# Other orders for the attention's steps, units and loads, a fourth buffer for k, and six units looked at, in a planned attention-and-MLP kernel

## The chip, the core and the metric

The kernel runs on one core of a Trainium2 chip. The metric is the device time of one execution in microseconds (us). A core has a matrix engine (TensorE, PE in the rows), a vector engine (VectorE, DVE), an activation engine (ScalarE, ACT), a general engine (GpSimd, POOL) and a sequencer that issues the transfers here (SyncE, SP). Each takes its own instructions in a fixed order, and waits on semaphores for the others and for DMAs.

## The reference

A decayed linear attention over 2 batches, 8 heads, 768 tokens of 64 numbers is followed by two MLP layers on 1536 tokens of 512 numbers:

```python
for b in range(nb):                         # blocks of the sequence
    intra = einsum('bhic,bhjc->bhij', qb, kb) * Dmask
    intra = einsum('bhij,bhjd->bhid', intra, vb)
    inter = einsum('bhid,bhde->bhie', qb * lam_pow, kv_state)
    out[:, :, sl] = intra + inter
    kv_state = lam_block * kv_state + einsum('bhsd,bhse->bhde', kb * rev_pow, vb)
x = out, heads side by side                 # 1536 x 512
g = x @ w_gate                              # 512 -> 1536
x = (g * sigmoid(g) * (x @ w_val)) @ w_out  # 1536 -> 512
h = x @ w_in                                # 512 -> 2048
return (h * cos(h)) @ w_out2                # 2048 -> 512
```

The MLP's weights are stored as float64.

## The kernel before

**Attention.** The tokens are taken in 12 chunks of 128 (6 for each batch), all heads at once. For chunk g TensorE runs these steps, built in `att_sub` (L1054): `t` transposes q and k in 64-row halves (L1079, 16 small matmuls); `s` makes the scores (L1097); `d` makes this chunk's share of the state from k and v (L1104); `a` multiplies masked scores with v (L1110); `c` adds the part from the state (L1119). `m` builds the decay mask once. Between them, ScalarE copies the transposes to `qkt` and the results to `xh`, VectorE multiplies the scores with the mask (`at`) and makes `xl`, the rest of x behind the rounding to `xh`, and GpSimd decays k (`kd`), q (`qd`) and the state (`stmp`). Chunks 5 and 11 need no `d`.

**MLP.** Every matmul of it is done as three, on high and low parts (`mm3`, L154 to L156). A `unit` is one of 12 x 512 columns: `gate` or `val`, a block of 512 tokens (0 to 2), and a slice f of the weights (`up_sub`, L1252). For f from 2 on, and for the second layer, blocks are done by a scheme of seven products (`product_sub`, L1281), in the order b, c, a, d, 2, 3, 4 (q and r for four 256x512 quarters of blocks 0 and 1; h and w for block 2, half as wide). Product d goes on in the PSUM bank of product c, after ScalarE has copied c out of it (`copy_job`, L1199). A `down` is a product with the second weight matrix, four pieces of three matmuls each (`down_subs`, L1474). Weights pass from DMA (`raw`) through ScalarE (`ct`) and VectorE (shift L198, join L205) to their parts `wh` (ScalarE) and `wl` (VectorE).

**Orders.** A planner, run when the kernel is built, gives each engine its next instruction by its own estimated times. During the attention TensorE's order is fixed by the string `STEPS` (L53), in which `u` stands for the next unit. After that `next_pe` (L623) takes the first piece of a down, or one of the first `LOOK` pieces of the list of units and products (L629), whichever can start soonest by its estimate. The loads of q, k, v and of the first weight slices (`G` gate, `V` val) are issued by SP in the order of `LOADS` (L58), as far as buffers (`BUFS`, L63) are free. `FETCHES` (L51) and `ATT_NS` (L49) are estimates alone. Where the planner expects TensorE to wait over 1000 ns in the attention, it puts zero matmuls (`zero`, L232; about one for each 115 ns) before the step. The list of units (L298) begins with gate of blocks 0 and 1, then val of both.

Of the kernel before, what the change touches and what calls it, by code (L numbers as in the profile page):

```python
# [26 lines left out]
GBUFS = (5, 0)  # L27
SBUFS, ZBUFS = (6, 1), 2
UNIT_BANKS = 2, 4
LOOK = 4  # L30
ZERO, ZERO_FROM = 115, 1000
COLD, COLD_TO = 215, 7500
KEPT = 4
# [14 lines left out]
EARLY = 4  # L48
LATENCY = 130  # L49
ISSUE = 400  # L50
STALL, FETCHES = 1000, (13000, 20600, 29000, 36500, 45000, 54500, 63500)  # L51
BEHIND = 7000
ATT_NS = {"t": 470, "mask": 700, "s": 892, "st": 464, "av": 875, "qs": 440}  # L53
TILES = {"mask": "32", "t": "64*128", "s": "64*128", "st": "128*64", "av": "128*64", "qs": "64*64"}
STEPS = (
# [3 lines left out]
)  # L59
LOADS = (  # L60
    "q0 k0 k1 q1 q3 k2 q4 q2 k3 q5 v0 k4 k6 k5 v1 v2 q6 k7 v3 v4 G0 v5 k8 q7 v6 q8 "
    "v8 v7 k9 q9 q10 k10 k11 q11 V0 v9 v11 v10 V1 G1"
)  # L63
HELD = 6, 7, 8, 9
BUFS = {"q": 3, "k": 3, "v": 5, "qkt": 2, "qd": 3, "kd": 2, "at": 2, "stmp": 2}
WARM = 4, 5


# [4 lines left out]
def kernel(  # L73
# [222 lines left out]
    ]  # L296
    first2 = len(downs)
    units = [(nm, blk, f) for f in range(GROUP1) for nm in ("gate", "val") for blk in range(NBLK - 1)]  # L298
    units += [(nm, NBLK - 1, f) for f in range(GROUP1) for nm in ("gate", "val")]
    parts = "bcad234"  # L300

# [45 lines left out]
    def matrix(kind, f):  # L347

        if kind in "qh":
            return tuple((nm, f) for nm in ("gate", "val", "sa", "sb"))  # L350
        return ("in2", f), ("in2", f + 1), ("ta", f), ("tb", f)

    def work(op):

        if op[0] in ATT_NS:
            return ATT_NS[op[0]] / 1360
        if op[0] in ("h", "w"):
# [14 lines left out]
    at, todo = 0, list(downs)  # L372
# [40 lines left out]
    for key in list(first_use):  # L413
        if key[0] in ("sa", "sb", "ta", "tb"):
            m = matrix("q" if key[0] in FIRST else "r", key[1])
# [18 lines left out]
    def up_mm(ps, nm, f, x):  # L434
# [15 lines left out]
        "ct": [(0, i) for i in range(CT)], "stage": [(0, i) for i in range(STAGE)], "ring": [(0, i) for i in free if i not in HELD],  # L450
        **{nm: [(0, i) for i in range(n)] for nm, n in BUFS.items()},
    }
# [148 lines left out]
    def turning():  # L601

        return "plain2" in when and ("r", 0, "3") not in when
# [3 lines left out]
    def switch(sub):  # L607

        kind = sub["op"][0]
        if TILES.get(kind) != last_tiles[0]:  # L610
            return SWITCH.get(kind, 145)
        return 60 if last_tiles[1] and kind not in ATT_NS else 0

    def small(sub):

        return sub["op"][0] in ("h", "w")
# [6 lines left out]
    def next_pe():  # L623
# [3 lines left out]
        if pe_att:  # L627
            ahead_ = min(ahead_, key=lambda e: e[1][0]["clock"]),
        for unit, subs in ahead_ if pe_att else ((False, pe_downs[:1]), (True, pe_units[:TURN[1] if turning() else LOOK])):  # L629
            for sub in subs:  # L630
# [12 lines left out]
    def run_pe(sub, end, idle):  # L643

        unit = any(sub is s for s in pe_units)
        last_small[0] = small(sub)
        last_tiles[:] = TILES.get(sub["op"][0]), sub["op"][0] in ATT_NS
        for subs in (pe_att, pe_units, pe_downs):
            subs[:] = [s for s in subs if s is not sub]
        items = []  # L650
        for _ in range(int(sub["bank"])):
# [3 lines left out]
            if unit:  # L655
                unit_banks.add(item[1])
        sub["fn"](*(items or [None]), **({"idle": idle} if idle and sub["op"][0] in ATT_NS and items else {}))
        for key in sub["keys"]:
# [395 lines left out]
    def att_sub(op):  # L1054
# [92 lines left out]

        return dict(ns=ATT_NS[kind], needs=needs, keys=[], bank=n, fn=fn, then=then, clock=seen[op], op=op)

# [513 lines left out]
```

## Time and profile before

| what | us |
|---|---|
| median of 3 runs (lowest, highest) | 591.8 (591.25, 592.13) |
| the profiled execution | 590.59 |
| its span | 588.8 |
| TensorE busy in the span | 578.5 (98%) |
| VectorE busy | 506.0 (86%) |
| ScalarE busy | 362.5 (62%) |
| GpSimd busy | 34.1 (6%) |

Busy time is a sum over the whole span. The attention takes about the first 64 us, and its loads hold the DMA engines busy for most of it; after that TensorE, VectorE and ScalarE work on the MLP alone. Where an engine waits is read from the list of waits and from the timeline, in which an idle time before an instruction stands in brackets with the engine that ended it.

### The profile page before, as it was taken

The page shows a single profiled execution, that of the slowest core. Times are in us where ns is not written, and L with a number is a line of the kernel's source. Part 1 is how long each engine was busy: PE and PEld are TensorE (multiplying, and loading weights), DVE is VectorE, ACT ScalarE, POOL GpSimd, SP SyncE. Part 2 cuts the span into 40 slices and gives each one's busy share as a digit, 9 for nine tenths or more (in the row PEclk, how much of TensorE's full clock was granted, in tenths as well). Part 3 has the DMA queues.
Part 4 walks back from the last instruction along what each step waited for, and adds up shares of the span by engine and source line. Part 5 has one row for each costly group of instructions (what it writes and reads, how often), then busy time and mean ns, then how long its engine had stood idle before and what let it go on. Part 6 is the DMA issues. An engine that isn't in the chain of part 4 may idle for free.

```text
span 588.8 us, 9643 instructions
## 1 busy us (share of the span) xinstructions
PE 578.5 (98%) x3620; PEld 491.8 (84%) x3620; DVE 506.0 (86%) x943; ACT 362.5 (62%) x689; POOL 34.1 (6%) x50
## 2 busy tenths in 40 slices
PE   8999999999999999999999999999999999989997
PEld 5888888888888888888888888888888888868886
DVE  4688899878889889786979999969799999999973
ACT  3554767757567557454453679876568667857641
POOL 5646000000000000000000000000000000000000
PEclk9999999999999999999999999999999999999999
DMA  9999362554585554543441522301212031300013
GB/s 189 211 210 212 113 147 71 162 144 147 175 225 185 156 146 140 170 128 141 129 142 51 180 89 72 107 2 39 70 37 71 1 108 37 108 0 1 1 74 141
DMA packets 72816, 66.68 MB, mean 113 GB/s; under 512 B 40002, under 2 KB 60738, under 8 KB 72770
## 3 DMA queue, kind: packets, MB, share of 16 engines
q1 hardware_dynamic: 72768, 66.07, 40.2%
q8 instruction: 28, 0.46, 0.3%
q14 instruction: 18, 0.15, 0.1%
q10 hardware_dynamic: 2, 0.00, 0.0%
HBM read 54.00 MB, written 12.06 MB: 112 GB/s over the span
## 4 chain that ended last, share of the span: by engine, by line
PE 84%; DVE 11%; ACT 2%; DMA 1%; issue 1%; SPq 0%; ACTq 0%; DVEq 0%
PE bank L154 21%; PE bank L155 21%; PE bank L156 20%; PE bank L1493 5%; PE bank L1494 5%; PE bank L1495 5%; DVE s L529 2%; DVE sum L529 2%; PE bank L1110 2%; PE bank L1097 2%; DVE wl L541 1%; DMA v<-in_v_dram 1%; PE bank L1119 1%; PE bank L1079 1%; PE bank L1104 1%; DVE s L1241 1%
## 5 line engine op out<-in xcount | busy, mean ns | idle before, releaser
L154 PE MATMUL bank<-xl,wh 128*128 128x512 f32 (+1 forms) x336 | 118.4, 352 | 3.0 <-ACT s L536 3.0
L536 ACT ACTIVATE s<-s 128x512 f32<-128x512 f32 (+2 forms) x124 | 73.4, 594 | 75.2 <-DVE s L529 47.5
L155 PE MATMUL bank<-xh,wh 128*128 128x512 f32 (+1 forms) x336 | 117.7, 350 | 0.0
L156 PE MATMUL bank<-xh,wl 128*128 128x512 f32 (+1 forms) x336 | 117.3, 349 | 0.0
L536 ACT ACTIVATE s<-bank 128x512 f32<-128x512 f32 (+2 forms) x126 | 62.5, 500 | 36.4 <-PE bank L156 30.8
L536 ACT ACTIVATE gh<-s 128x512 fp32r<-128x512 f32 x84 | 52.7, 628 | 38.7 <-DVE s L529 35.3
L529 DVE TENSOR_TENSOR s<-bank,s 128x256 f32<-128x256 f32 (+1 forms) x102 | 57.3, 563 | 22.2 <-PE bank L156 21.3
L154 PE MATMUL bank<-wl,gh 128*128 128x512 f32 (+1 forms) x196 | 75.6, 386 | 0.0
L155 PE MATMUL bank<-wh,gh 128*128 128x512 f32 (+1 forms) x196 | 75.6, 386 | 0.0
L156 PE MATMUL bank<-wh,gl 128*128 128x512 f32 (+1 forms) x196 | 75.5, 385 | 0.0
L154 PEld LDWEIGHTS bank<-xl,wh 128*128 128x128 f32 x336 | 63.6, 189 | 12.7 <-ACT s L536 3.7
L156 PEld LDWEIGHTS bank<-xh,wl 128*128 128x128 f32 x336 | 63.6, 189 | 8.4
L155 PEld LDWEIGHTS bank<-xh,wh 128*128 128x128 f32 x336 | 63.7, 190 | 8.1
L529 DVE TENSOR_TENSOR sum<-bank,sum 128x512 f32<-128x512 f32 (+1 forms) x97 | 63.2, 681 | 8.1 <-PE bank L156 5.8
L536 ACT ACTIVATE wh<-ct 128x512 fp32r<-128x512 f32 x91 | 55.5, 627 | 23.8 <-DVE ct L205 20.2
L541 DVE TENSOR_TENSOR wl<-ct,wh 128x512 fp32r<-128x512 f32 x91 | 61.3, 688 | 6.9 <-ACT wh L536 6.2
L529 DVE TENSOR_TENSOR gl<-s,gh 128x512 fp32r<-128x512 f32 x84 | 57.7, 689 | 6.3 <-ACT gh L536 5.9
L1493 PE MATMUL bank<-gh,wl 128*128 128x512 f32 x144 | 56.2, 390 | 0.0
L1494 PE MATMUL bank<-gh,wh 128*128 128x512 f32 x144 | 56.2, 390 | 0.0
L1495 PE MATMUL bank<-gl,wh 128*128 128x512 f32 x144 | 56.1, 389 | 0.0
L193 ACT ACTIVATE ct<-raw 128x512 f32<-128x512 f32 x68 | 44.9, 668 | 7.6 <-DMA raw<-in_moe_w_out_dram 4.4
L205 DVE SCALAR_TENSOR_TENSOR ct<-ct,raw 128x512 int32<-128x512 int32 x68 | 46.4, 689 | 3.1 <-ACT ct L193 1.3
(169 smaller groups left out, 1034.7 us busy)
## 6 DMA issues: line engine op xcount, KB each, us to landing
raw<-in_moe_w_out_dram SPq DMA_DIRECT2D x28, 512.0 KB, 3.6
raw<-in_moe_w_in_dram SPq DMA_DIRECT2D x16, 512.0 KB, 3.8
raw<-in_moe_w_gate_dram SPq DMA_DIRECT2D x24, 256.0 KB, 4.6
raw<-in_moe_w_val_dram SPq DMA_DIRECT2D x24, 256.0 KB, 4.5
draftout<-raw SPq DMA_DIRECT2D x9, 512.0 KB, 2.6
q<-in_q_dram SPq DMA_DIRECT2D x12, 256.0 KB, 5.2
k<-in_k_dram SPq DMA_DIRECT2D x12, 256.0 KB, 5.3
v<-in_v_dram SPq DMA_DIRECT2D x12, 256.0 KB, 5.7
```

Source lines behind the costliest of these rows:

```text
L154: nc.tensor.matmul(ps, wh, xl, start=first, stop=False, **kw)
L155: nc.tensor.matmul(ps, wh, xh, start=False, stop=False, **kw)
L156: nc.tensor.matmul(ps, wl, xh, start=False, stop=last, **kw)
L193: nc.scalar.activation(t, words[:, :, 1].bitcast(F32), AF.Prelu, scale=2.0 ** -112, alpha=2.0 ** 32)
L205: nc.vector.scalar_tensor_tensor(out=w, in0=w, scalar=3, in1=lo, op0=ALU.logical_shift_left, op1=ALU.bitwise_or)
L529: engine, 66 + n * 1.047 if engine == "DVE" else n * 2.45, lambda: unit.tensor_tensor(out=out, in0=in0, in1=in1, op=op),
L536: return go("ACT", (175 if fn == AF.Silu else 40) + n * 0.94, lambda: nc.scalar.activation(out, src, fn, **kw))
L541: return "any", {"DVE": 66 + n * 1.047, "POOL": n * 2.45}, lambda e: (nc.vector if e == "DVE" else nc.gpsimd).tensor_tensor(out=out, in0=i ...
L1097: nc.tensor.matmul(ps[:, p * C:(p + 1) * C], kt[r, p, :], qt[r, p, :], start=True, stop=True)
L1493: nc.tensor.matmul(ps, lo[:, cs], gh, start=first, stop=False)
L1494: nc.tensor.matmul(ps, hi[:, cs], gh, start=False, stop=False)
L1495: nc.tensor.matmul(ps, hi[:, cs], gl, start=False, stop=last)
```

## The change

`BUFS` gives k four buffers; `LOOK` is six; the first four units become gate and val of block 0, then gate and val of block 1, all with f = 0; `STEPS`, `LOADS` and the estimates have other values. No instruction is added or taken away on VectorE, ScalarE or GpSimd; TensorE has 25 zero matmuls in two places of the attention instead of 26 in one, beside 14 at its start in both.

```diff
-LOOK = 4
+LOOK = 6
...
-STALL, FETCHES = 1000, (13000, 20600, 29000, 36500, 45000, 54500, 63500)
+STALL, FETCHES = 1000, (12560, 18624, 25014, 34517, 41507, 53380, 61826, 69630)
...
-ATT_NS = {"t": 470, "mask": 700, "s": 892, "st": 464, "av": 875, "qs": 440}
+ATT_NS = {"t": 490, "mask": 700, "s": 892, "st": 464, "av": 875, "qs": 440}
...
-    "t0 m s0 t1 a0 t2 s1 d0 s2 d1 a1 t3 t4 a2 s3 d2 c2 c1 d3 a3 d4 c3 t5 s4 t6 s5 "
-    "a4 s6 a5 c4 c5 t7 a6 d6 u s7 t8 d7 d8 a7 t9 s8 c7 s9 t10 a8 u c8 t11 s10 a9 d9 "
-    "s11 c9 u d10 a10 a11 c10 c11"
+    "t0 m s0 t1 t2 s1 a0 d0 s2 t3 d1 a1 c1 a2 s3 t4 c2 a3 d2 d3 t5 s4 c3 s5 d4 a4 "
+    "t6 u c4 t7 s6 a5 s7 d6 c5 a6 a7 d7 c7 u u t8 u t9 s8 u t10 s9 d8 a8 t11 s10 "
+    "d9 a9 s11 u c8 c9 a10 d10 a11 c10 c11"
...
-    "q0 k0 k1 q1 q3 k2 q4 q2 k3 q5 v0 k4 k6 k5 v1 v2 q6 k7 v3 v4 G0 v5 k8 q7 v6 q8 "
-    "v8 v7 k9 q9 q10 k10 k11 q11 V0 v9 v11 v10 V1 G1"
+    "q0 k0 k1 q2 q1 v0 k2 q3 k4 k3 v1 v2 q4 v3 k5 q5 G0 v4 q6 k6 v5 k7 q7 V0 v6 v7 "
+    "k9 v9 k8 q8 G1 q10 k10 q9 v8 k11 q11 V1 v11 v10"
...
-BUFS = {"q": 3, "k": 3, "v": 5, "qkt": 2, "qd": 3, "kd": 2, "at": 2, "stmp": 2}
+BUFS = {"q": 3, "k": 4, "v": 5, "qkt": 2, "qd": 3, "kd": 2, "at": 2, "stmp": 2}
...
+    units[:4] = [(nm, blk, 0) for blk in range(2) for nm in ("gate", "val")]
```

The order of SP's first loads before (they are q0, k0 and k1, q1, k2, q2 and q3, v0 and v1, q4, k3 and k4, v2, q5):

```order
L936 DMA q<-in_q_dram 128x8x64
L936 DMA k<-in_k_dram 128x8x64 x2
L936 DMA q<-in_q_dram 128x8x64
L936 DMA k<-in_k_dram 128x8x64
L936 DMA q<-in_q_dram 128x8x64 x2
L936 DMA v<-in_v_dram 128x8x64 x2
L936 DMA q<-in_q_dram 128x8x64
L936 DMA k<-in_k_dram 128x8x64 x2
L936 DMA v<-in_v_dram 128x8x64
L936 DMA q<-in_q_dram 128x8x64
```

And in the change (q0, k0 and k1, q2 and q1, v0, k2, q3, k3, v1, k4, v2, q4):

```order
L937 DMA q<-in_q_dram 128x8x64
L937 DMA k<-in_k_dram 128x8x64 x2
L937 DMA q<-in_q_dram 128x8x64 x2
L937 DMA v<-in_v_dram 128x8x64
L937 DMA k<-in_k_dram 128x8x64
L937 DMA q<-in_q_dram 128x8x64
L937 DMA k<-in_k_dram 128x8x64
L937 DMA v<-in_v_dram 128x8x64
L937 DMA k<-in_k_dram 128x8x64
L937 DMA v<-in_v_dram 128x8x64
L937 DMA q<-in_q_dram 128x8x64
```

v0 moves from the eighth place to the sixth, k2 from the fifth to the seventh and q1 from the fourth to the fifth; further on v3, q5, the two loads of G0 and v4 hold places 14 and 16 to 19, and V0, G1 and V1 stand earlier than before among the rest.

ScalarE late in the second layer, before: `s_5886<-bank5_5827` copies product c of f = 12 (r_c_12 below) out of its bank; the two `gh` rows ahead of it round results that VectorE has multiplied.

```order
L1245 ACTIVATE s_5710<-s_5710,halfpi_86 128x512
L536 ACTIVATE wh_5855<-ct_5825 128x512
L536 ACTIVATE s_5768<-s_5768 128x512
L536 ACTIVATE s_5867<-s_5699 128x512
L1245 ACTIVATE s_5768<-s_5768,halfpi_86 128x512
L536 ACTIVATE gh_5870<-s_5710 128x512
L536 ACTIVATE gh_5887<-s_5768 128x512
L536 ACTIVATE s_5886<-bank5_5827 128x512
```

The same copy in the change is `s_5790<-bank0_5782`:

```order
L193 ACTIVATE ct_5793<-raw_5547 128x512
L537 ACTIVATE s_5778<-s_5405 128x512
L537 ACTIVATE s_5790<-bank0_5782 128x512
L537 ACTIVATE gh_5791<-s_5678 128x512
L537 ACTIVATE s_5694<-s_5694 128x512
```

The copy moves ahead of the next `gh`; on TensorE the products between r_c_12 and r_d_12 change from w_d, w_2, r_a and w_3 to eight pieces of downs and r_a.

## Rows read from the trace of the kernel before

**Rows 1.** Page part 1: busy us (share of span) x instructions.
```profile
PE 578.5 (98%) x3620; PEld 491.8 (84%) x3620; DVE 506.0 (86%) x943; ACT 362.5 (62%) x689; POOL 34.1 (6%) x50
```

**Rows 2.** Waits of TensorE: line, releaser, us in total, times, longest.
```profile
PE bank L154 <- ACT s L536: 3.0, 2, 2.9
PE bank L1110 <- DMA v<-in_v_dram: 1.5, 1, 1.5
PE bank L1097 <- ACT qkt L536: 1.2, 3, 0.6
PE bank L234 <- DVE halfpi L1602: 1.1, 1, 1.1
PE bank L1088 <- DVE skewed L269: 0.2, 1, 0.2
```

**Rows 3.** Timeline of TensorE in the attention: start, us, line, operation, idle before.
```profile
9.16 3.01 PE L234 MATMUL bank<-zeros 128*128 128x256 bf16 x26
13.62 1.09 PE L1110 MATMUL bank<-at,v 128*64 128x128 f32 x16 [1.45 <-DMA v<-in_v_dram]
14.65 0.46 PE L1079 MATMUL bank<-anti,q 64*128 64x64 f32 x8
15.19 1.11 PE L1097 MATMUL bank<-qkt 64*128 64x128 f32 x16
16.24 0.69 PE L1104 MATMUL bank<-v,kd 128*64 128x64 f32 x16
...
28.15 1.11 PE L1097 MATMUL bank<-qkt 64*128 64x128 f32 x16
```

**Rows 4.** Timeline of SP's issues: start, us, what, how many.
```profile
3.81 1.22 SPq L936 DMA_DIRECT2D k<-in_k_dram  x1
5.07 2.20 SPq L936 DMA_DIRECT2D q<-in_q_dram  x2
...
21.99 1.05 SPq L936 DMA_DIRECT2D k<-in_k_dram  x1
```

**Rows 5.** Page part 6: issues, KB each, median us to landing.
```profile
k<-in_k_dram SPq DMA_DIRECT2D x12, 256.0 KB, 5.3
v<-in_v_dram SPq DMA_DIRECT2D x12, 256.0 KB, 5.7
```

**Rows 6.** Timeline of TensorE: a unit alone among steps, and the step after it.
```profile
57.43 0.50 PE L154 MATMUL bank<-xl,wh 128*128 128x512 f32 x1
...
60.38 0.69 PE L1104 MATMUL bank<-v,kd 128*64 128x64 f32 x16
```

**Rows 7.** Timelines of VectorE, ScalarE and TensorE around the longest wait.
```profile
514.37 1.13 DVE L529 TENSOR_TENSOR s<-bank,s 128x512 f32<-128x512 f32 x2
515.42 0.68 DVE L541 TENSOR_TENSOR wl<-ct,wh 128x512 fp32r<-128x512 f32 x1
516.02 0.68 DVE L529 TENSOR_TENSOR s<-s 128x512 f32<-128x512 f32 x1
...
516.74 0.63 ACT L536 ACTIVATE gh<-s 128x512 fp32r<-128x512 f32 x1 [0.81 <-DVE s L529]
517.27 0.58 ACT L536 ACTIVATE s<-bank 128x512 f32<-128x512 f32 x1
...
517.90 0.50 PE L154 MATMUL bank<-xl,wh 128*128 128x512 f32 x1 [2.86 <-ACT s L536]
```

**Rows 8.** Windows: stretch, us; busy (x) of PE, PEld, DVE, ACT, POOL; PEclk, DMA, GB/s.
```profile
66.60:88.40 21.80, 21.80 (x98) 18.04 (x97) 21.59 (x41) 15.45 (x29) 0.00 (x0) 1.00 0.57 144
...
453.60:512.70 59.10, 59.10 (x302) 50.58 (x301) 57.83 (x105) 40.98 (x75) 0.00 (x0) 1.00 0.20 63
...
60.40:101.50 41.10, 41.10 (x251) 34.44 (x251) 40.19 (x76) 29.92 (x55) 0.00 (x0) 1.00 0.43 116
...
500.00:585.00 85.00, 82.14 (x411) 69.90 (x411) 73.40 (x126) 50.48 (x91) 0.00 (x0) 1.00 0.15 53
585.50:588.80 3.30, 0.00 (x0) 0.00 (x0) 0.37 (x1) 0.00 (x0) 0.00 (x0) 0.89 0.18 61
```

## Prediction, made before the change was timed

> **What bounds the kernel now.** I read the page's busy shares first. TensorE is busy for 578.5 of 588.8 us, 98% [rows 1], so the change can win little but TensorE's own waits, and VectorE at 86% is the one other engine close enough to make new ones. Then the list of TensorE's waits [rows 2]: 1.45 us for v0, 1.2 us for ScalarE's copies of the transposes in three places, 3.0 us for a ScalarE copy in two places (2.9 of it in one), and 1.3 us at the start that no edit touches. The timeline of the attention adds what the list can't show [rows 3]: ahead of a0 stand 26 zero matmuls, 3.01 us, that compute nothing, 0.116 us each. Waits and zeros after the first steps together are 3.01 + 1.45 + 1.2 + 3.0 = 8.7 us; that is the most the change could give. Last, the windows [rows 8]: from 60.4 to 101.5 us VectorE is busy for 40.19 of 41.10 us, and before the long wait, 453.6 to 512.7, for 57.83 of 59.10. In these two places VectorE, not TensorE, is what a new order can run into.
>
> **The front: steps and loads.** a0 waited because v0 was the eighth load. In the change it is the sixth, and t2 and s1 come ahead of a0. What counts now is k2, the seventh load. I take the n-th load of the change to be issued when the n-th was before, and to land after the median of its kind. The seventh was issued in the second half of a row from 5.07 that lasts 2.20 us, so at about 6.2 [rows 4], and lands at 6.2 + 5.3 = 11.5 us [rows 5]. On TensorE t1 began before at 9.16 - 0.59 = 8.57 (a t takes 0.54 to 0.59; 14.65 to 15.19 [rows 3]). Now q1 is the fifth load, issued at 3.81, landing at 9.1: t1 starts 0.5 us later. Then 15 zeros (1.74 us) run to 9.1 + 0.59 + 1.74 = 11.4, and t2 starts at 11.5 with 0.1 us of wait.
>
> From there to the next zeros I compare sets of steps. Before, t2 starts at 14.65 and s4 at 28.15: 13.5 us, with 0.6 us of waits in it (1.2 less the longest, 0.6, which comes later). The change's steps from t2 to s5 are the same set plus s4, s5 and a0, less d4: with s 1.05 (15.19 to 16.24), a 1.03 (13.62 to 14.65) and d 0.6 (a bit under its 0.69), 13.5 - 0.6 + 2.1 + 1.0 - 0.6 = 15.4 us. s5 ends at 26.9. There the change has 10 zeros, 1.16 us, ahead of d4, to 28.1; v4 is the nineteenth load (two of G0 stand before it), issued at 21.99, landing at 21.99 + 5.7 = 27.7. The zeros cover it. Each other load of the stretch lands within about half a microsecond of its step by the same count, on either side (v2: issued near 13.2, landing at 18.9; a2 due at 18.4), so I take 0.5 us for small waits, between 0 and 1.6. The waits for `qkt` (1.2 us) go: between each t and its s the new string has at least two other steps, and on ScalarE's queue the copies stand ahead of the copies of x, which were what held them. A fourth k buffer takes away the wait of k3's load for GpSimd's kd0; that is worth nothing by itself while the transfers are what is full.
>
> The units cost something. One alone among small steps takes 60.38 - 57.43 = 2.95 us [rows 6]; in a row, 21.8 / 8 = 2.72 [rows 8]. Before there were three lone ones and the run that ends the attention, now five runs and the last: 2 x 0.23 = 0.46 us. They also move VectorE's work on them forward, into the stretch before 60 us where it is less full; I count that as cover, not as gain.
>
> Sum of the front: gone 3.01 + 1.45 + 1.2 = 5.7; new 0.5 + 1.84 + 1.16 + 0.5 + 0.46 = 4.5. Gain 1.2 us, between -0.3 (all small waits at their upper end, and half of the `qkt` waits kept) and 1.8.
>
> **The long wait: LOOK and the order of products.** The chain of this wait is in three timelines [rows 7]. Product w_3 of f = 12 is done at about 514.8. VectorE then runs the sum of w_3, a `wl` and a multiply (514.37 to 516.70, back to back); ScalarE's `gh` needs the multiply and starts at 516.74; behind it in ScalarE's order stands the copy of r_c_12's bank (517.27), and r_d_12, which goes on in that bank, starts at 517.90 after 2.86 us. The copy itself needed nothing: r_c_12 was long done. It stood behind a `gh`. In the change the copy stands right behind r_c_12's end in ScalarE's order, ahead of the next `gh`, and on TensorE eight pieces of downs and r_a, 8 x 0.68 + 1.36 = 6.8 us, lie between r_c_12 and r_d_12 (0.68 and 1.36 are 3 and 6 matmuls of 2.72 / 12). So this wait goes. What is late next is VectorE: in the order of the change, from the end of down (1, block 2, f = 7) to the multiply that frees the bank for r_a_12, 101 VectorE instructions stand. 81 of them have 512 columns, 0.60 us each (515.42 to 516.02 [rows 7]); 20 are half as wide or shifts, 0.34 by their share of that: 55.4 us. TensorE has 57 us of matmuls in the same stretch. I find no stretch in the second layer with less than 1 us to spare, so I take 0.2 us of wait there, up to 1.5 if VectorE loses what it lost before (59.10 - 57.83 = 1.3). Gain 2.86 - 0.2 = 2.7; the small wait of 0.1 stays.
>
> **The stretch after the attention.** With six looked at, the products h_b, h_c, h_a of f = 2 come before the first downs, so q_2 of f = 2 is due 4.5 us earlier in time (3.4 of it by order, 1.1 by the front). By the order, VectorE has 4.0 us less to do before it (67.9 us in all instead of 71.9). Since VectorE is full there [rows 8], 0.5 us of its spare is used. Before, TensorE never waited for it there [rows 2]; how much was to spare these rows don't tell. I take no cost, and up to 1 us if its first 60 us hold more idle time than before.
>
> **Sum.** 1.2 + 2.7 = 3.9, less 0.1 for that last risk: 3.8 us. The profiled execution took 590.59 us, 1.8 us more than its span, 1.2 us under the median; from 590.59 it gives 586.8, and for the median 591.8 - 3.8 = 588.0.
>
> **Rivals.**
> 1. The front gives nothing: loads land later than my count and the small waits reach their upper end. For it: the loads are paced so that each lands at its step. Against it: with the fourth buffer k3 is issued without waiting. Time 588.0 + 1.5 = 589.5.
> 2. The long wait only moves: VectorE has 55.4 of 57 us to do, and losing 3 us there in place of 1.3 makes r_a_12 wait 1.7 us or more; with a second such place, the whole 2.7 come back. Against it: the copy no longer depends on VectorE. Time 588.0 + 2.7 = 590.7.
> 3. Slower: a load in the middle of the queue waits for its buffer, and SP, which issues in order, holds all behind it. The place is q11 (its buffer is q8's, free after t8), with v11, v10 and the first gate slice of f = 2 behind; and v4. TensorE then waits at d4, t9 or t11. It decides from 3.8 + 1.2 = 5 us of new waits, about four loads' worth (36 loads of the front lie in some 50 us). For it: nothing in the attention covers a wait. Against: t8 is due near 47 and q11's place near 46, so 2 us at most. Time from 593.0 on, 594 taken.
> 4. The clock. Granted clock is 1.00 (2.4 GHz) in the window that holds the wait of 2.86 us, and 0.89 over the 3.3 us after the last matmul, so it falls to the lower level (1.2 GHz) only behind longer idleness [rows 8]. If v4 left TensorE idle beyond 2.86 us, 1.7 us more than planned, the first unit at half the clock would cost 2.95 us more, and little is left of the gain: 588.0 + 1.7 + 2.95 = 592.7. The Trainium skill (TensorE: Matmul & The Clock Gate, Part 1, "What's actually happening") says that the slow clock is the default and only activity lifts it; by that rule fewer zeros speak against this change. The trace agrees that idleness brings the fall, but shows none after 2.86 us.
>
> **Chances.** Forecast 0.62 (586.8 to 589.0); rival 1 0.15; rival 2 0.13; rival 3 0.06; rival 4 0.04. The range has to leave out no more than 2 in 10: from 586.4 (front at its best) to 590.8, which takes in rivals 1 and 2. About 0.2%, 1.2 us, is what a measurement of this kernel can tell from no change: faster is below 590.6, slower above 593.0. Forecast, rival 1 and a third of rival 2 are faster: 0.81; two thirds of rival 2 and half of rival 4 the same: 0.11; the rest slower: 0.08.
>
> **What would show it.** Right: the zeros before t2 end at 11 to 12 us with almost no wait; TensorE's list has no entry over 1 us but the start; the last of the twelve units ends near 87.2 instead of 88.4; r_d_12 without a wait. Wrong: a wait for DMA at d4, a2, t9 or t11 over 1 us (rivals 1 and 3); a wait for VectorE at r_a_12 or in the first 20 us after the units (rival 2); a granted clock under 1.00 before the last matmul (rival 4).

## The result, and the profile after

| | median, us | lowest to highest | runs |
|---|---|---|---|
| before | 591.96 | 591.25 to 592.46 | 4 |
| the change | 586.72 | 586.43 to 587.32 | 4 |

The ratio is 0.9911, with a 95% interval of 0.9895 to 0.9926: 5.2 us less, where 3.8 were predicted. The two profiled executions, 590.59 and 586.67 us, differ by 3.9 us. So the medians moved 1.3 us further than the profiles, and the experiments have to say why.

The page of the change, part 1 (as [rows 1]):

```profile
PE 578.7 (99%) x3619; PEld 491.2 (84%) x3619; DVE 502.9 (86%) x943; ACT 364.3 (62%) x689; POOL 34.5 (6%) x50
```

Its list of TensorE's waits (as [rows 2]):

```profile
PE bank L234 <- DVE halfpi L1603: 1.1, 1, 1.1
PE bank L1080 <- DMA q<-in_q_dram: 0.6, 1, 0.6
PE bank L1111 <- DMA v<-in_v_dram: 0.4, 1, 0.4
PE bank L1089 <- DVE skewed L269: 0.2, 1, 0.2
```

TensorE is busy for as long as before, 578.7 against 578.5 us, in a span that is 4.1 us shorter. The waits of [rows 2] for ScalarE, 3.0 us in the MLP and 1.2 in the attention, are gone; what is left after the start are 1.0 us for two loads. Behind the attention the list has nothing.

TensorE in the attention of the change (start, us, line, operation, idle before), beside [rows 3]; the last row is the first product of f = 2, q_b_2, right behind the twelve units:

```profile
9.69 1.81 PE L234 MATMUL bank<-zeros 128*128 128x256 bf16 x15
11.43 0.46 PE L1080 MATMUL bank<-anti,q 64*128 64x64 f32 x8
...
22.15 1.09 PE L1111 MATMUL bank<-at,v 128*64 128x128 f32 x16 [0.40 <-DMA v<-in_v_dram]
...
24.81 0.53 PE L1080 MATMUL bank<-anti,q 64*128 64x64 f32 x8 [0.63 <-DMA q<-in_q_dram]
...
28.16 1.27 PE L234 MATMUL bank<-zeros 128*128 128x256 bf16 x10
29.35 0.69 PE L1105 MATMUL bank<-v,kd 128*64 128x64 f32 x16
...
34.74 0.67 PE L1120 MATMUL bank<-qd,state 64*64 64x128 f32 x16
...
88.15 0.39 PE L154 MATMUL bank<-xl,wh 128*128 128x512 f32 x1
```

t2 starts at 11.43, s5 ends at 28.16, d4 starts at 29.35, and the units end at 88.15, where they ended at 88.40 before [rows 8]. In this execution the front won 0.2 us.

ScalarE's copy of r_c_12's bank in the change, and r_d_12 on TensorE, which answer to [rows 7]:

```profile
505.02 0.60 ACT L537 ACTIVATE s<-bank 128x512 f32<-128x512 f32 x1
505.51 0.62 ACT L537 ACTIVATE gh<-s 128x512 fp32r<-128x512 f32 x1
...
511.62 0.39 PE L154 MATMUL bank<-xl,wh 128*128 128x512 f32 x1
```

The copy is done 6 us before r_d_12 needs it, and r_d_12 follows its forerunner without a gap.

The last matmul on TensorE, before and in the change:

```profile
585.13 0.28 PE L156 MATMUL bank<-wh,gl 128*128 128x256 f32 x1
...
580.91 0.28 PE L156 MATMUL bank<-wh,gl 128*128 128x256 f32 x1
```

So the profiles' 3.9 us are: 0.2 at the front, 3.0 of waits in the MLP, and 1.0 that nobody had counted: from the start of q_b_2 to the start of the last matmul, less the waits, TensorE takes 493.7 us before (585.13 - 88.40 - 3.0) and 492.8 in the change (580.91 - 88.15). From there to the end, and outside the span, the change takes 0.3 us longer.

### The profile page after: what moved, and what is told of

Read it like the earlier page. It is cut to its first block, busy times and chain, and to the rows that moved or that the text cites. A ratio compares the mean times of both kernels' runs of the same rounds, so it can differ in the third digit from the quotient of the medians.

```text
span 584.7 us, 9694 instructions
## 1 busy us (share of the span) xinstructions
PE 578.7 (99%) x3619; PEld 491.2 (84%) x3619; DVE 502.9 (86%) x943; ACT 364.3 (62%) x689; POOL 34.5 (6%) x50
## 4 chain that ended last, share of the span: by engine, by line
PE 97%; DMA 1%; DVE 1%; POOL 0%; issue 0%; DVEq 0%
PE bank L154 25%; PE bank L156 24%; PE bank L155 24%; PE bank L1495 6%; PE bank L1494 6%; PE bank L1496 6%; PE bank L1098 2%; PE bank L1111 2%; DMA q<-in_q_dram 1%; PE bank L1080 1%; PE bank L1120 1%; PE bank L1105 1%; PE bank L234 1%; POOL powers L266 0%; PE bank L1089 0%
## 5 line engine op out<-in xcount | busy, mean ns | idle before, releaser
L530 DVE TENSOR_TENSOR sum<-bank,sum 128x512 f32<-128x512 f32 (+1 forms) x97 | 62.9, 681 | 11.5 <-PE bank L156 8.9
L530 DVE TENSOR_TENSOR s<-bank,s 128x512 f32<-128x512 f32 (+1 forms) x102 | 57.1, 563 | 16.6 <-PE bank L156 14.7
```

Source lines behind the costliest of these rows:

```text
L530: engine, 66 + n * 1.047 if engine == "DVE" else n * 2.45, lambda: unit.tensor_tensor(out=out, in0=in0, in1=in1, op=op),
```

## Experiments

### Each part alone

The kernel before with `LOOK = 6` alone:

```diff
-LOOK = 4
+LOOK = 6
```

> The kernel before with LOOK = 6 and nothing else changed. Theory (LOOK is what takes the long wait away): ahead of r_d_12 TensorE has w_4 of f = 12 (256 columns) and r_b of f = 14 more than before, 2.1 us of products, so that its wait of 2.86 us falls to about 0.7; the attention keeps its 26 zeros and its waits for v and qkt. 1.5 to 2.1 us faster than before, about 590.2. Rival (the order of units and steps took it away, and LOOK is worth nothing): the wait stands as long as it was or stands elsewhere, 592.0 within 0.6.

Measured: 588.48 us (588.23 to 588.62), before 592.4 when timed beside it, ratio 0.9944 (0.9926 to 0.9963). The place of the long wait on TensorE:

```profile
517.80 0.50 PE L154 MATMUL bank<-xl,wh 128*128 128x512 f32 x1 [0.78 <-ACT s L536]
```

The wait is 0.78 us, as the 2.1 us of products put ahead of r_d_12 let one expect, and r_d_12 starts at the same time as before (517.80, 517.90 before). From profile to profile the gain is 2.4 us (590.59 to 588.23), a little over the expected 1.5 to 2.1; from median to median it is 3.9. That is the same surplus as in the result.

The change with `LOOK = 4`:

```diff
-LOOK = 6
+LOOK = 4
```

> The changed kernel with LOOK = 4 and the rest of the change. Theory (the steps, units and loads alone shift the plan so that r_c_12's copy is no longer behind a gh): r_d_12 has no wait, as in the change; but by a count of VectorE's instructions a product of f = 2 in the second layer, near 365 us, comes 3 us too early for VectorE: one new wait of 2 to 3 us there, 589 to 590 where the change has 586.7. Rival 1 (LOOK does nothing): no wait over 1 us, 586.7 within 0.6. Rival 2 (LOOK took the long wait away): 2.9 us of wait at r_d_12 near 514 us, 589.6.

Measured: 590.8 us (589.63 to 593.63), ratio 0.9983 (0.9966 to 1.0001). TensorE near 365 us, and the windows from there on (columns as in [rows 8]):

```profile
361.70 0.50 PE L154 MATMUL bank<-xl,wh 128*128 128x512 f32 x1 [0.93 <-DVE s L530]
...
365.31 0.50 PE L154 MATMUL bank<-xl,wh 128*128 128x512 f32 x1 [1.95 <-DVE s L530]
```

```profile
364.00:365.00 1.00, 0.00 (x0) 0.00 (x0) 1.00 (x3) 0.44 (x2) 0.00 (x0) 1.00 0.00 0
365.00:366.00 1.00, 0.69 (x3) 0.61 (x4) 1.00 (x3) 1.00 (x3) 0.00 (x0) 1.00 0.00 0
366.00:367.00 1.00, 1.00 (x5) 0.81 (x4) 1.00 (x3) 0.65 (x2) 0.00 (x0) 0.72 0.00 0
367.00:368.00 1.00, 1.00 (x4) 0.71 (x3) 1.00 (x3) 1.00 (x2) 0.00 (x0) 0.50 0.00 0
368.00:369.00 1.00, 1.00 (x4) 0.81 (x3) 1.00 (x2) 0.05 (x1) 0.00 (x0) 0.50 0.00 0
```

r_d_12 has no wait here. So the new steps, units and loads alone clear that place, but the wait only moves: VectorE, busy for all of each window from 360 to 370 us, comes 0.93 and 1.95 us late for two products of the second layer. And behind that TensorE's granted clock is 0.50, its lower level of 1.2 GHz; it falls between 366 and 367 us, when TensorE has been at work again for about a microsecond. Three of the twelve runs show a mean granted clock of 0.997; they are the three longest, and this profile is of one of them.

The change with `LOOK = 5`:

```diff
-LOOK = 6
+LOOK = 5
```

> The changed kernel with LOOK = 5. Theory (a fifth piece looked at is enough for the product that fills the place; by a count of VectorE's instructions no product of the second layer comes too early, unlike with LOOK = 4): no wait over 1 us behind the attention, no run with a lower clock, 586.7 within 0.6. Rival (the gain hangs on just this plan, and each other number of pieces makes a wait of its own): a wait of 1 us or more at some product, 588 or more.

Measured: 586.30 us (585.92 to 586.46), ratio 0.9899 (0.9883 to 0.9916), clock 0.999 to 1.00 in all runs, and after the start no wait but 1.1 us for loads of q. So the plan of the change is not one lucky case; with these steps a fifth piece is enough. With 0.9911 for the change, the two can't be told apart.

The four corners together, medians in us:

| steps, loads, units, k buffers | LOOK 4 | LOOK 6 |
|---|---|---|
| as before | 592.4 | 588.5 |
| as in the change | 590.8 | 586.7 |

LOOK is worth 3.9 to 4.1 us, the rest 1.6 to 1.8. The last corner was timed in another series than the other three, and the 1.6 at LOOK = 4 is not clear of noise (ratio up to 1.0001). What the new steps and the new loads do apart from each other was not tried.

### What the long wait waited for

The prediction said that r_c_12's copy "needed nothing" and only stood behind a `gh` in ScalarE's order. One ScalarE instruction moved, ahead of that `gh`; behind r_d_12 the planner then orders the rest anew:

```diff
-spawn(copy_job(kind, f, nm, *live[...]), seen[op], t)
+spawn(copy_job(kind, f, nm, *live[...]), seen[op] - (30 if op == ("r", "c", 12) else 0), t)
```

> The kernel before with one ScalarE instruction moved: the copy of r_c_12's bank ahead of the second gh, one place earlier; everything up to there as before. Theory (the wait is that of a copy which stands behind a gh in ScalarE's order): r_d_12 starts 1.2 to 1.5 us earlier, its wait falls from 2.86 to about 1.4; by a count of VectorE's instructions up to 0.6 us of it is given back at a later product, so 0.8 to 1.5 us faster than before, about 590.8. Rival (VectorE or the bank holds r_d_12, and the copy is only the last thing seen): the wait stays 2.5 us or more, 592.0 within 0.5.

Measured: 592.07 us (590.05 to 593.42), ratio 0.9998 (0.9984 to 1.0013). VectorE, ScalarE and TensorE at the place:

```profile
516.49 0.68 DVE L529 TENSOR_TENSOR s<-s 128x512 f32<-128x512 f32 x1
...
517.21 0.60 ACT L536 ACTIVATE s<-bank 128x512 f32<-128x512 f32 x1 [0.81 <-DVE s L529]
517.70 0.62 ACT L536 ACTIVATE gh<-s 128x512 fp32r<-128x512 f32 x1
...
517.86 0.79 PE L154 MATMUL bank<-xl,wh 128*128 128x512 f32 x1 [2.35 <-ACT s L536]
```

The copy now stands ahead of the `gh`, and still starts only when VectorE's multiply ends (516.49 + 0.68 = 517.17). The wait fell by 0.5 us, to 2.35, not by 1.5, and the time is that of before. My theory falls: the `gh` was not what held the copy. In the code a copy first takes one of six `s` buffers (`copy_job`, L1199), and that multiply is what gives one back. At r_c_12's copy the planner has no `s` buffer free; two `ct` buffers of the same size are.

So the copy gets a `ct` buffer, for this one product:

```diff
+        if (kind, f, nm) == ("r", 12, "c"):
+            i = yield "take", "ct"
+            s, i = word_tile(i), ("ct", i)
+        else:
             i = yield "take", "s"
             s = s_tile(i)
...
     def give(pool, i, t):
+        if isinstance(i, tuple):
+            pool, i = i
```

> The kernel before with one buffer more for one copy: r_c_12's copy goes to a `ct` buffer that stands free there, instead of waiting for one of the six `s` buffers. Up to r_c_12 all is as before. Theory (the copy, and with it r_d_12, waited for the `s` buffer that VectorE's multiply frees): the copy runs right behind r_c_12, r_d_12 has no wait, by a count of VectorE's instructions no later product waits in its place, and no run has a lower clock: 2.8 us less than the fast group of before (590.6 to 591.1), so 587.8 to 588.3, some 4 us under before's median. Rival (VectorE is simply behind with its work there): 2 us or more of wait come back within the next 40 us, 590 or more.

Measured: 588.06 us (588.03 to 588.55), before 592.33, ratio 0.9942 (0.9928 to 0.9955). ScalarE's copy and r_d_12 in it:

```profile
512.29 0.60 ACT L538 ACTIVATE ct<-bank 128x512 f32<-128x512 f32 x1 [1.38 <-PE bank L156]
...
513.73 0.50 PE L154 MATMUL bank<-xl,wh 128*128 128x512 f32 x1
```

The copy waits for TensorE's r_c_12 alone, 1.38 us, and r_d_12 has no wait. With the copy done early, the planner also puts r_d_12 ahead of r_a and w_3. One buffer for one product is worth as much as LOOK = 6 in the whole kernel, and no wait comes back later. The cause of the long wait is settled: the six `s` buffers, through VectorE that frees them.

### What a wait costs beside its length

The kernel before, profiled once more:

> The kernel before, once more, for a second profile of it. Theory: if the execution takes 592 us or more, the granted clock is 0.50 for some 3 us behind r_d_12's wait and the products there take twice as long, and the attention is as before within 0.5 us; if it takes under 591.2, the clock is 1.00 throughout. Rival (the slower executions lose their time in the loads of the attention): the first product of f = 2 starts later than 89.5 us in an execution of 592 us or more.

Measured: 592.37 us. TensorE behind the long wait, and the windows:

```profile
518.22 0.79 PE L154 MATMUL bank<-xl,wh 128*128 128x512 f32 x1 [2.87 <-ACT s L536]
518.81 0.63 PE L155 MATMUL bank<-xh,wh 128*128 128x512 f32 x1
519.24 0.63 PE L156 MATMUL bank<-xh,wl 128*128 128x512 f32 x1
```

```profile
517.00:518.00 1.00, 0.00 (x0) 0.00 (x0) 1.00 (x3) 0.95 (x2) 0.00 (x0) 0.96 0.00 0
518.00:519.00 1.00, 0.78 (x2) 0.69 (x3) 1.00 (x3) 0.68 (x2) 0.00 (x0) 0.50 0.00 0
519.00:520.00 1.00, 1.00 (x4) 0.80 (x3) 0.90 (x2) 0.54 (x1) 0.00 (x0) 0.50 0.00 0
520.00:521.00 1.00, 1.00 (x4) 0.72 (x3) 0.91 (x2) 0.83 (x3) 0.00 (x0) 0.50 0.00 0
521.00:522.00 1.00, 1.00 (x5) 0.83 (x4) 0.00 (x0) 0.97 (x2) 0.00 (x0) 0.83 0.00 0
```

The wait is the same as in [rows 7], 2.87 against 2.86 us, but here the clock goes to 1.2 GHz, and matmuls start 0.43 us apart (518.81 to 519.24) instead of 0.23. r_d_12 takes 2.72 instead of 1.50 us and the step behind it 0.2 more: 1.4 us. The front is 0.35 us later than in the first profile (q_b_2 at 88.74). The two make up the 1.8 us by which this execution is longer.

Over 60 runs of the kernel before, timed beside these experiments, the mean granted clock of a run sorts the times: 20 runs with 0.999 or 1.00 take 590.6 to 591.5 us (median 591.0), 35 with 0.996 or 0.997 take 592.0 to 593.4 (median 592.4), and 5 with 0.994 take 593.2 to 594.8. So in two runs of three the clock falls somewhere, and the one of them that was profiled shows it behind this wait.

To show that the wait is the cause, ten matmuls that repeat r_d_12's first one into a free bank fill it, with nothing else moved on any engine:

```diff
+            if op == ("r", "d", 12):
+                spare = bank_tile(min(stock["bank"])[1])
+                for _ in range(10):
+                    nc.tensor.matmul(spare, w[0][:, 0:P], x[0][:, 0, :], start=True, stop=True)
```

> The kernel before with ten matmuls more, ahead of r_d_12, that repeat its first one into a free bank and whose result nobody reads: 10 x 0.23 = 2.3 us of work inside the wait of 2.86 us, all else in the same order. Theory (the wait costs twice, since in most executions the clock falls to its lower level behind it, for some 1.5 us): r_d_12 starts when it did, the clock stays at 1.00 in every run, and the runs lie at 590.5 to 591.2 where those of before lie at 590.6 to 594.8: 1.2 us under the median of before. Rival (the lower clock in runs of before has another cause than this wait): runs with a granted clock of 0.996 remain, median within 0.5 of before's.

Measured: 590.84 us (590.53 to 591.18), ratio 0.9982 (0.9973 to 0.9991). The place on TensorE:

```profile
515.12 2.50 PE L1314 MATMUL bank<-xh,wh 128*128 128x512 f32 x10
518.14 0.51 PE L154 MATMUL bank<-xl,wh 128*128 128x512 f32 x1 [0.53 <-ACT s L536]
```

r_d_12 starts no earlier, at 518.14. Yet none of twelve runs has a lower clock (14 of the 22 of before that were timed beside them do), and the median falls by 1.5 us. Work that nobody needs is worth 1.5 us here, because it keeps the clock; and since no run shows the lower clock once the wait is filled, it needs no cause beside this wait.

### The front

The change with zeros only from 1500 ns of expected waiting, which was to take out the ten ahead of d4 and nothing else:

```diff
-ZERO, ZERO_FROM = 115, 1000
+ZERO, ZERO_FROM = 115, 1500
```

> The changed kernel without the ten zeros ahead of d4 (zeros only from 1500 ns of expected waiting, so that those ahead of t2 stay). Theory (v4 has landed when the zeros begin or just after, so that they are idle work on the path): d4 starts 1.0 to 1.2 us earlier, 585.6. Rival 1 (TensorE then waits for v4 or for the next load as long as the zeros took): 586.7 within 0.4. Rival 2 (the zeros keep the clock): granted clock under 1.00 behind the gap, the first unit 2.9 us longer, 588.5 or more.

Measured: 587.37 us (586.35 to 587.82), ratio 0.9922 (0.9904 to 0.9940), no gain. TensorE in it:

```profile
2.60 1.25 PE L234 MATMUL bank<-zeros 128*128 128x256 bf16 x5
...
12.07 0.46 PE L1080 MATMUL bank<-anti,q 64*128 64x64 f32 x8
...
27.58 0.69 PE L1105 MATMUL bank<-v,kd 128*64 128x64 f32 x16
...
30.10 0.46 PE L1080 MATMUL bank<-ident,k 64*128 64x64 f32 x8 [0.33 <-DMA k<-in_k_dram]
...
31.85 0.50 PE L156 MATMUL bank<-xh,wl 128*128 128x512 f32 x1 [0.42 <-DVE wl L542]
...
34.37 0.67 PE L1120 MATMUL bank<-qd,state 64*64 64x128 f32 x16
```

The edit took out more than it was meant to: at the start of the kernel, ahead of t0, there are five zeros here and ten in the change, and t2 starts at 12.07 instead of 11.43. So the median, 0.65 us above the change's and outside the 0.4 of rival 1, doesn't price the ten zeros alone. The trace tells what becomes of them: d4 starts at 27.58, 1.77 us earlier than in the change's profile, but c4, behind the first unit, starts at 34.37 instead of 34.74. The lead is given back at t6, which waits for k6, and in the first unit, which waits for its weights: what follows in the load queue is just in time too. That is the mechanism of rival 1.

The change with three k buffers:

```diff
-BUFS = {"q": 3, "k": 4, ...}
+BUFS = {"q": 3, "k": 3, ...}
```

> The changed kernel with three k buffers instead of four, the rest as in the change. Theory of the prediction (the fourth buffer is worth nothing by itself while the transfers are full): 586.7 within 0.6. Rival (with these orders k3's load waits for GpSimd's kd0, and all loads of SP's queue behind it; the planner expects that and puts 56 zeros, 6.5 us, ahead of t3 and the first unit): 3 to 6 us slower than the change, 590 to 593, with the zeros before t3 in the timeline.

Measured: 589.39 us (588.91 to 590.74), ratio 0.9964 (0.9952 to 0.9976). SP's issue of k3 in the change and here, and TensorE's zeros before t3 here:

```profile
8.57 1.10 SPq L937 DMA_DIRECT2D k<-in_k_dram  x1
...
14.73 1.02 SPq L937 DMA_DIRECT2D k<-in_k_dram  x1
...
15.43 4.87 PE L234 MATMUL bank<-zeros 128*128 128x256 bf16 x43
20.22 0.46 PE L1080 MATMUL bank<-anti,q 64*128 64x64 f32 x8
```

The rival holds in its mechanism, though its 3 to 6 us were too much: the fourth buffer is worth 2.7 us with these orders. With three, k4, which stands ahead of k3 in `LOADS`, takes the buffer that comes free first; k3's load is issued at 14.73 us instead of 8.57, lands at 20.28, and 43 zeros fill the time. Of the 4.7 us by which t3 is late (20.22 against 15.51) 2 are won back behind it.

The change with the old list of units:

```diff
-    units[:4] = [(nm, blk, 0) for blk in range(2) for nm in ("gate", "val")]
```

> The changed kernel with the old list of units (gate of blocks 0 and 1, then val of both), the rest as in the change. Theory (the order of units goes with the new steps: gate of block 1 stands where val of block 0 stood, and block 1's x is not yet made): the planner expects 2.3 us of waiting before that unit, so 2 to 3 us slower than the change, 588.7 to 589.7, with one wait of that size at the second unit. Rival (the order of units alone is worth nothing, since x is ready): 586.7 within 0.6.

Measured: 589.19 us (588.14 to 590.66), ratio 0.9947 (0.9930 to 0.9964). TensorE's second unit:

```profile
46.20 0.50 PE L154 MATMUL bank<-xl,wh 128*128 128x512 f32 x1 [2.11 <-DVE xl L529]
```

As expected: block 1's `xl` isn't made when its gate comes second. The new list of units is what the new steps need, and worth 2.5 us with them; what it would do with the old steps wasn't tried. One of its eight runs has a lower clock.

The change, profiled once more:

> The changed kernel, once more, for a second profile of its front. Theory (the front gains little, whatever the execution): the first product of f = 2 starts within 0.6 us of 88.15, with 0.5 to 1.5 us of waits for loads between t2 and the first unit. Rival (the first profile had an unlucky front): it starts at 87.4 or earlier.

Measured: 585.81 us. TensorE in it:

```profile
24.08 0.53 PE L1080 MATMUL bank<-anti,q 64*128 64x64 f32 x8 [0.61 <-DMA q<-in_q_dram]
...
27.43 1.27 PE L234 MATMUL bank<-zeros 128*128 128x256 bf16 x10
28.63 0.69 PE L1105 MATMUL bank<-v,kd 128*64 128x64 f32 x16
...
87.37 0.39 PE L154 MATMUL bank<-xl,wh 128*128 128x512 f32 x1
```

q_b_2 starts at 87.37, as the rival wanted. But that the first profile had an unlucky front doesn't follow: its 586.67 us lie in the middle of the four runs of the result (586.43 to 587.32), and this execution is shorter than all of them. With LOOK = 5, whose attention is the same, q_b_2 starts at 87.48; with LOOK = 4, also the same, at 89.88. Six executions with the attention of before give 88.37 to 89.21, the middle 88.68; the four with that of the change 87.37 to 89.88, the middle 87.8. So the front gains about 0.9 us by these middles, from executions that spread by more than that. The runs at full clock give an estimate of 0.6: before and change differ by 591.0 - 586.7 = 4.3 us, and with the parts of the result, 3.0 for the waits in the MLP, 1.0 for the steps behind the front and -0.3 for the end, that is what is left.

## Why the prediction was right, and where it was not

**Direction and size.** Faster was right, and 3.8 us is close to the 3.9 by which the profiles differ. The median of the change, 586.72, lies 1.3 us under the 588.0 predicted and just inside the range.

**The front, point by point.** t2 at 11.5 us: 11.43 and 11.38 in the two profiles. t1 half a microsecond later, then 15 zeros: so. s5's end at 26.9: 28.16 and 27.43. d4 at 28.1: 29.35 and 28.63. The end of the units at 87.2: 88.15 and 87.37. The step that was too small is "0.5 us for small waits": a3 and t5 alone waited 1.03 us in the first profile, and in part the first unit's weights were late. The prediction's 1.2 us of gain stand against 0.2 in the first profile, some 0.6 by the runs at full clock and about 0.9 in the middle of ten executions. The lower end of its range for the front doesn't come out of its own terms: 1.2, less 1.1 more of small waits and 0.6 for half of the `qkt` waits, is -0.5, not -0.3. The zeros ahead of d4, which were to "cover" v4, cost nothing that could have been kept: the lead without them was down to 0.4 us by c4.

**The fourth buffer "is worth nothing by itself".** Wrong: 2.7 us. I asked what the buffer gives the old order, and not what the new order does without it, where k4 is to be loaded ahead of k3. The new list of units I didn't price at all (the 0.46 us are for units that stand alone among the steps): with the old list the new steps lose 2.5 us.

**The long wait.** That it goes, and 2.7 us with it, was right, and so was the bound by VectorE: no wait took its place in the change. The cause was wrong. I read the copy's place behind a `gh` as its reason; the copy waited for an `s` buffer, as the moved copy and the spare buffer show. The heading "LOOK and the order of products" put two causes in one; apart, each clears the place or nearly so, but with the new steps alone the wait comes back at 365 us. Rival 2 described that, for another product (r_a_12), and it is what LOOK prevents.

**The clock.** The term that was missing. From one profile I took that the clock "falls to the lower level only behind longer idleness" than 2.86 us. That profile speaks against it already, at its end (columns as in [rows 8]):

```profile
588.00:588.80 0.80, 0.00 (x0) 0.00 (x0) 0.00 (x0) 0.00 (x0) 0.00 (x0) 0.55 0.00 0
```

The last matmul ends at 585.13 + 0.28 = 585.41, and a mean of 0.55 over these 0.8 us means a fall at about 588.1, after 2.7 us of idleness. And in two executions of three it fell behind just that wait, and cost 1.4 us more (592.4 against 591.0). The median of before contains this, its profile did not, and I carried the profile's difference over to the median. The Trainium skill (TensorE: Matmul & The Clock Gate, Part 1, "What's actually happening") says that the slow clock is the default, which activity lifts; the second profile of before agrees, with 0.50 behind 2.87 us of idleness, and so does the filled wait, with 1.00.

**The shorter steps.** 1.0 us, not foreseen. In before, r_b_2, r_d_0, w_3 of f = 12 and r_d_12 each took 0.14 to 0.17 us longer than others of their kind; they are the neighbours of the two waits of [rows 2]. That makes 0.6 us; a wait costs a little on both sides. The other 0.4 is spread over steps that I can't assign.

**The sum in hindsight.** Waits 3.0, shorter steps 1.0, clock 1.4 in most runs, less 0.3 at the end: 5.1 us. With 0.2 to 0.9 for the front, the 592.4 of the later runs of before come to 586.4 to 587.1, where the change has 586.7 and its sister with LOOK = 5 has 586.3. The two terms that the prediction lacked, the clock and the shorter steps, took the median down to the lower end of the range; had the front given its 1.2 us as well, it would have lain below it. That the median stayed inside is luck.

## What to carry to other kernels

Before a wait is blamed on the instruction ahead in the queue, ask which buffer the waiting instruction takes and who frees it; one buffer more in the right place was worth as much here as a new order of everything. A wait of TensorE may cost more than it lasts, and only in some executions: look at the granted clock of all runs, not of the profiled one alone, before its price is set. And price each part of a change both against the old kernel and as the one part missing from the new.

## What the hardware showed that was not expected

- The kernel with the wait of 2.86 us kept its clock in 20 of 60 runs and had it lowered in 40; with a wait of 2.35 us (the moved copy) it was lowered in 8 of 12, and with 0.93 and 1.95 us close together in 3 of 12. In the three profiles that show the lower level it stayed for a little over 3 us; in the second profile of before that cost 1.4 us.
- With the same orders, the end of the units moved between 87.37 and 89.88 us from one execution to another. Most of it is waiting for loads: the listed waits for them in the attention sum to 1.0 us in the earliest and 2.8 us in the latest.
